# Attention pairs of two batches in one chain with joined biases, w2's splits at other places of a visit, and an opening with its loads and squares in another order

## The chip, the cores and the metric

One core of a Trainium2 chip runs the whole kernel. The metric is the device time of one execution in microseconds (us). The engines are PE (TensorE, matmuls), DVE (VectorE), ACT (ScalarE), POOL (GpSimd) and SP, which issues nearly all DMAs. Each engine works through its own instructions in program order and waits for the others by semaphores.

## What is computed

Random-feature attention for 4 batches of 8 heads (576 positions, 64 dimensions, 128 features), followed by a mixture of 4 experts on the 2304 x 512 result:

```
phi(x) = exp(x omega' - |x|^2/2 - max(...)) / sqrt(m)      x = q, k scaled by 64^-1/4
kv = phi(k)' v,   z = sum phi(k),   attn = phi(q) kv / (phi(q) z + 1e-6)
out = sum over e of p[:, e] * (relu(attn w1[e]) w2[e])     w1: 512x1024, w2: 1024x512
```

All arithmetic is float32. For the expert matmuls each operand is split into two parts, high and low, and three matmuls (high·high, low·high, high·low) make one product.

## The kernel before

**Order by hand.** The emission order of the code is the order on each engine. A tile pool hands out rotating buffers; a tile's buffer is reused when its last emitted reader is done. PSUM has 8 banks in one pool (`bank`), used by everything.

**Batch 0** of the attention is done in `begin` (four head pairs, class `Pair`) and finished in `first_rest`. **Batches 1 to 3** are done by class `Halves`, one pair of heads at a time, by the generator `later_ticks`, cut into ticks. The expert work is a list of visits: half an expert (4 blocks of 128 hidden features, FH = 4) for a range of rows. The first 11 visits (N0 = 11) are on the rows of batch 0 (`first_visit`, `plain`): three for 256 rows, five for 512 rows and, between them, three more for 256 rows. Then 16 visits (`fast`) work on two blocks of 896 rows, 8 visits each; they form the hidden layer with seven products p1 to p7 for each of two groups, 14 products of six 128x448 matmuls, then seven output tiles of 12 matmuls 128x512.

**Pace.** A visit yields shares of work ("units"): 8 for a visit of 512 or 896 rows, 4 for one of 256. `emit` runs ticks of the window's generator at a fixed rate per unit. Window 0 (visits 0 to 2) runs `first_rest` at 14/11 ticks a unit. Window 3 (visits 3 to 10, 52 units) runs batches 1 and 2 at 107/45.4 = 2.36. Window N0 (first 8 fast visits, 64 units) runs batch 3 at 53/(64 x 0.86) = 0.96. In a fast visit all 14 products and the start of three output tiles are one unit, so no tick falls between products.

**A pair's 12 ticks.** 1: project k (two banks `k_ps`), project the tails of k and q (two banks `t_ps`), maxima of k. 2: bias of k (two small DVE operations on 128x8, L293 and L294), four exponentials on ACT (`exp`, L300), lengths of q. 3: four more exponentials, maxima of the tails (L286). 4: project q, bias of k's and q's tails (L293, L294 on 128x1), exponentials of the tails (`exp_tails`, L308), maxima of q. 5, 6: bias and exponentials of q. 7: `sum_keys`, whose first matmul (L317) needs the tail of k. 8 to 12: transposes, numerators, divisions. Loads and squares of the next pair are spread over ticks 5 to 10. In front of a batch's first pair stand 5 opening ticks: loads of k, q, v and the tails of v, an empty tick, the squares on POOL, the lengths on DVE.

**w2.** `load("w2")` brings 128x512 of w2 into one of three buffers `w2r`; `split_w2` makes the high part `w2h` on ACT (L473) and the low part `w2l` on POOL (L476), and then issues the next load on SP. In `begin` two loads are issued ahead, so the loads stay two ahead of the splits for good. `sides` splits w1 for the next visit in the output tiles and issues its loads.

**omega.** `om_r`, a copy of omega for batches 1 to 3, is loaded on SP late in `begin` and scaled on DVE (L901) in the middle of batch 0's last steps.

Of the kernel before, what the change touches and what calls it, by code (L numbers as in the profile page):

```python
# [6 lines left out]
F32 = mybir.dt.float32  # L7
# [7 lines left out]
def attention_moe(ctx, tc, kT, qT, kd, qd, kn, qn, vn, omT, probs, w1, w2, out):  # L15
# [10 lines left out]
    nc = tc.nc  # L26
# [209 lines left out]
    class Halves(Pair):  # L236
# [42 lines left out]
            for j in range(2):  # L279
                nc.vector.tensor_reduce(mx[:, 4 * j:4 * j + 4], ps[j].rearrange("p (i m) -> p i m", m=M), AX.X, ALU.max)  # L280

        def maxima_tails(self):
            for i, which in enumerate("kq"):
                for j in range(2):
                    rows = slice(j * D, (j + 1) * D)
                    nc.vector.tensor_reduce(  # L286
                        getattr(self, "mx" + which)[rows, 8:], self.t_ps[j][rows, i * M:(i + 1) * M], AX.X, ALU.max
                    )

        def bias(self, which, cs):  # L290

            sq, mx, nb = (getattr(self, x + which)[:, cs] for x in ("sq", "mx", "nb"))
            nc.vector.scalar_tensor_tensor(mx, sq, -QS * QS / 2, mx, ALU.mult, ALU.add)  # L293
            nc.vector.scalar_tensor_tensor(nb, sq, -QS * QS / 2, mx, ALU.mult, ALU.subtract)  # L294

# [4 lines left out]
                nc.scalar.activation(f[:, i], ps[:, i * P:(i + 1) * P], AF.Exp, bias=nb[:, 4 * j + i:4 * j + i + 1])  # L300
            (self.kp if which == "k" else self.qx)[j] = f

        def exp_tails(self):
            for i, which in enumerate("kq"):
                f = att.tile([P, 1, M], F32, tag=which + "pt", name=which + "p", bufs=2)
                for j in range(2):
                    rows = slice(j * D, (j + 1) * D)
                    nc.scalar.activation(  # L308
                        f[rows, 0], self.t_ps[j][rows, i * M:(i + 1) * M], AF.Exp, bias=getattr(self, "nb" + which)[rows, 8:]
                    )  # L310
                (self.kp if which == "k" else self.qx)[2] = f

        def sum_keys(self):

# [58 lines left out]
                    own = slice(j * D, (j + 1) * D)  # L373
                    nc.vector.tensor_tensor(raw_x[own, place(self.hp), c:c + m], ps[j][own, o:o + m], dn[own, o:o + m], ALU.mult)

    def later_ticks(b):

        pairs = [Halves(b, hp) for hp in range(NP)]
        pairs[0].load("k")
        pairs[0].load("q")  # L380
        pairs[0].load_v()
        pairs[0].load_tails()
        yield
        yield
        pairs[0].square("k")
        yield
        pairs[0].square("q")
        yield
        pairs[0].lengths("k")
        yield  # L390
        for p, then in zip(pairs, pairs[1:] + [None]):
            p.project("k")
            p.project_tails()
            p.maxima("k")
            yield
            p.bias("k", slice(0, 8))
            p.exp("k", 0)
            p.lengths("q")
            yield
            p.exp("k", 1)  # L400
            p.maxima_tails()
            yield
            p.project("q")
            p.bias("k", slice(8, 9))
            p.bias("q", slice(8, 9))
            p.exp_tails()
            p.maxima("q")
            yield
            p.bias("q", slice(0, 8))
            p.exp("q", 0)  # L410
            if then:
                then.load("k")
            yield
            p.exp("q", 1)
            if then:
                then.load("q")
            yield
            p.sum_keys()
            if then:
                then.load_v()  # L420
                then.square("k")
            yield
            p.turn(0)
            yield
            p.turn(1)
            if then:
                then.square("q")
            yield
            p.numerators(0)
            if then:  # L430
                then.lengths("k")
            yield
            p.divide(0)
            p.numerators(1)
            yield
            p.divide(1)
            yield
# [240 lines left out]
    def fast(v):  # L678

        u, n = visits[v][0], BIG // 2  # L680
        tiles = BIG // P
        hs = [tuple(held([P, 2 * n], x) for x in ("hh", "hl")) for _ in range(FH)]
        P_ = [{}, {}]
        ready = sides(v + 1) if v + 1 < len(visits) else iter(())
        more = build(u + 1) if u == 1 and visits[v + 1][0] == 2 else iter(())

        def product(g, p, where, start=True):
            if start:
                P_[g][where] = bank("g1")[:, :n]
            ps = P_[g][where]  # L690
            (wa, wc), (xa, xc) = W[v, "w1", g][p], X[p]
            for k in range(2):
                w = slice(k * P, (k + 1) * P)
                for a, x, at in ((wa, xa, 0), (wa, xc, 1), (wc, xa, 2)):
                    nc.tensor.matmul(  # L695
                        ps, a[:, w], x[:, k], start=(start and k + at == 0), stop=(k == 1 and at == 2), skip_group_check=not start
                    )

        def keep(g, where, name):
            P_[g][name] = t = held([P, 512], "sum", F32)[:, :n]  # L700
            nc.scalar.activation(t, P_[g][where], AF.Copy)  # L701

        def both(g, f, j, where, name):
            ha, hc = (x[:, j * n:(j + 1) * n] for x in hs[2 * g + f])
            t = P_[g][name]
            nc.vector.tensor_tensor(t, P_[g][where], t, ALU.add)  # L706
            nc.scalar.activation(ha, t, AF.Relu)  # L707
            nc.vector.scalar_tensor_tensor(hc, t, 0.0, f32(ha), ALU.max, ALU.subtract)  # L708

        def p1(g):  # L710
            product(g, 1, "u")
            keep(g, "u", "p1")

        def p2(g):
            product(g, 2, "b2")
            both(g, 0, 0, "b2", "p1")

        def p5(g):
            product(g, 5, "b5")
            keep(g, "b5", "p5")  # L720

        def p6(g):
            product(g, 6, "u", start=False)
            keep(g, "u", "u2")

        def p7(g):
            product(g, 7, "u", start=False)
            both(g, 1, 1, "u", "p5")

        def p4(g):  # L730
            product(g, 4, "u", start=False)
            ha, hc = (x[:, :n] for x in hs[2 * g + 1])
            nc.scalar.activation(ha, P_[g]["u"], AF.Relu)
            nc.vector.scalar_tensor_tensor(hc, P_[g]["u"], 0.0, f32(ha), ALU.max, ALU.subtract)

        def p3(g):
            product(g, 3, "b5", start=False)
            both(g, 0, 1, "b5", "u2")

        g2 = {}  # L740

        def begun(t):
            g2[t] = bank("g2")
            outputs(v, hs, g2[t], t, range(2))

        p1(0)
        split_w2()
        p2(0)
        split_w2()
        p5(0)  # L750
        next(more, None)
        p6(0)
        split_w2()
        p1(1)
        next(more, None)
        p2(1)
        split_w2()
        p7(0)
        next(more, None)
        p5(1)  # L760
        p3(0)
        p4(0)
        next(more, None)
        p6(1)
        next(ready, None)
        begun(0)
        p7(1)
        next(more, None)
        begun(1)
        p3(1)  # L770
        p4(1)
        next(more, None)
        begun(2)
        yield 1
        for t in range(tiles):
            if t in g2:
                outputs(v, hs, g2[t], t, range(2, FH))
            else:
                g2[t] = bank("g2")
                outputs(v, hs, g2[t], t, range(FH))  # L780
            gather(v, g2[t], t)
            next(ready, None)
            next(more, None)
            yield 1
        for _ in more:
            pass

    def begin():
# [84 lines left out]
        keys(3)  # L873
        load("w2")
        load("w2")
        for _ in range(4):
            split_w(nc.gpsimd, nc.gpsimd)
        for p in ps:
# [7 lines left out]
        ps[2].exp("q", 0)  # L886
        ps[3].project("q", 0)
        keys_exp(3)
        for p in ps[:2]:
            p.square("q1", nc.gpsimd)  # L890
        for _ in range(4):
            split_w(nc.gpsimd, nc.gpsimd)

        ps[0].finish(0)
        ps[1].numerators(0)
# [2 lines left out]
        ps[3].exp("q", 0)  # L898

        normalize_probs()  # L900
        nc.vector.tensor_scalar(om_r, om_r, QS, None, ALU.mult)  # L901
        ps[1].finish(0)
        ps[2].numerators(0)
        ps[3].turn(0, nc.vector)
# [25 lines left out]
            split_w(lo=nc.vector)  # L930
            yield 1

    def first_rest(pairs):

        pairs[0].project("q", 1)
        pairs[0].project("q", 2)
# [1 line left out]
        for hp, p in enumerate(pairs):  # L938
# [4 lines left out]
            if hp + 1 < NP:  # L943
                pairs[hp + 1].project("q", 1)
                pairs[hp + 1].project("q", 2)
            yield
            p.turn(1, nc.vector)
            p.turn(2, nc.vector)
            yield
            p.numerators(1)  # L950
            yield
            p.finish(1)
        yield

    def chain(*many):
        for x in many:
            yield from x
# [2 lines left out]

    def emit():
        pairs, g1 = begin()
        windows = {
            0: (first_rest(pairs), 14 / 11),
            3: (chain(later_ticks(1), later_ticks(2)), 107 / 45.4),
            N0: (later_ticks(3), 53 / (NV * (BIG // P + 1) * 0.86)),
        }
        ticks, n, done, per = iter(()), 0, 0.0, 0
        for v in range(len(visits)):
# [70 lines left out]
```

## Time and profile before

| | us |
|---|---|
| median of 3 runs | 946.17 (946.09 to 950.82) |
| the profiled execution's own time | 950.79 |
| its span, first to last instruction | 949.0 |
| PE busy | 912.3 (96%) |
| DVE busy | 571.9 (60%) |
| ACT busy | 433.1 (46%) |
| POOL busy | 379.7 (40%) |
| mean granted clock of TensorE | 0.991 |

A busy PE is one that has a matmul under way; its clock is granted at 2.4 GHz (1.0) or 1.2 GHz (0.5), and a mean between them over a stretch is a mix of the two.

### The profile page before, as it was taken

The page shows a single profiled execution, that of the slowest core. Times are in us where ns is not written, and L with a number is a line of the kernel's source. Part 1 is how long each engine was busy: PE and PEld are TensorE (multiplying, and loading weights), DVE is VectorE, ACT ScalarE, POOL GpSimd, SP SyncE. Part 2 cuts the span into 40 slices and gives each one's busy share as a digit, 9 for nine tenths or more (in the row PEclk, how much of TensorE's full clock was granted, in tenths as well). Part 3 has the DMA queues.
Part 4 walks back from the last instruction along what each step waited for, and adds up shares of the span by engine and source line. Part 5 has one row for each costly group of instructions (what it writes and reads, how often), then busy time and mean ns, then how long its engine had stood idle before and what let it go on. Part 6 is the DMA issues. An engine that isn't in the chain of part 4 may idle for free.

```text
span 949.0 us, 13220 instructions
## 1 busy us (share of the span) xinstructions
PE 912.3 (96%) x4892; PEld 784.8 (83%) x4892; DVE 571.9 (60%) x993; ACT 433.1 (46%) x964; POOL 379.7 (40%) x296
## 2 busy tenths in 40 slices
PE   7799998998999989999999999999999999999998
PEld 7788787877877868888888888888788888888886
DVE  5464577767887846648486576677535545545443
ACT  5354565545666445444534435353443343342430
POOL 3736444353543434332343524244344343343330
PEclk9999999999999989999999999999999999999999
DMA  6534535255331333121311302114022031021102
GB/s 169 143 112 145 157 117 184 71 155 164 126 129 34 97 103 114 59 67 26 125 56 59 126 5 85 35 54 155 24 78 68 23 89 66 24 89 56 45 12 77
DMA packets 47361, 83.56 MB, mean 88 GB/s; under 512 B 8705, under 2 KB 17089, under 8 KB 47297
## 3 DMA queue, kind: packets, MB, share of 16 engines
q1 hardware_dynamic: 47056, 82.43, 28.1%
q8 instruction: 38, 0.62, 0.3%
q10 hardware_dynamic: 240, 0.30, 0.1%
q14 instruction: 27, 0.21, 0.1%
HBM read 77.99 MB, written 4.72 MB: 87 GB/s over the span
## 4 chain that ended last, share of the span: by engine, by line
PE 59%; DVE 4%; issue 2%; ACT 1%; DMA 1%; POOL 1%; SPq 0%; ACTq 0%; POOLq 0%
PE g L695 26%; PE g L579 10%; PE g L581 10%; PE g L580 10%; DMA w2r<-in_w 1%; DVE acc L592 1%; PE kv L321 1%; POOL w1sl L476 1%; PE qt_ps L332 0%; DVE sum L706 0%; DVE xbl L476 0%; DVE dn L370 0%; DVE mxk L293 0%; ACT xbh L473 0%; PE k_ps L266 0%
## 5 line engine op out<-in xcount | busy, mean ns | idle before, releaser
L579 PE MATMUL g<-w2h,hh 128*128 128x512 f32 x536 | 213.1, 397 | 1.9 <-ACT hh L570 1.0
L581 PE MATMUL g<-w2h,hl 128*128 128x512 f32 x536 | 209.8, 391 | 0.5 <-DVE hl L571 0.5
L580 PE MATMUL g<-w2l,hh 128*128 128x512 f32 x536 | 209.2, 390 | 0.0
L476 POOL TENSOR_TENSOR w2l<-w2r,w2h 128x512 fp32r<-128x512 f32 x93 | 122.9, 1328 | 142.0 <-ACT w2h L473 100.0
L476 POOL TENSOR_TENSOR w1sl<-w1r,w1sh 128x1024 fp32r<-128x1024 f32 (+1 forms) x59 | 113.4, 1922 | 159.9 <-ACT w1sh L473 158.6
L476 POOL TENSOR_TENSOR w1al<-w1r,w1ah 128x256 fp32r<-128x256 f32 (+1 forms) x77 | 82.2, 1085 | 164.4 <-ACT w1ah L473 162.3
L706 DVE TENSOR_TENSOR sum<-g,sum 128x448 f32<-128x448 f32 x96 | 59.7, 622 | 126.5 <-PE g L695 109.6
L592 DVE SCALAR_TENSOR_TENSOR acc<-g,pr,acc 128x512 f32<-128x512 f32 x126 | 93.9, 747 | 64.8 <-PE g L581 63.8
L581 PEld LDWEIGHTS g<-w2h,hl 128*128 128x128 f32 x536 | 100.6, 188 | 24.4 <-DVE hl L571 1.9
L579 PEld LDWEIGHTS g<-w2h,hh 128*128 128x128 f32 x536 | 101.0, 188 | 22.9 <-ACT hh L570 1.7
L580 PEld LDWEIGHTS g<-w2l,hh 128*128 128x128 f32 x536 | 100.9, 188 | 18.5
L707 ACT ACTIVATE hh<-sum 128x448 fp32r<-128x448 f32 x96 | 55.5, 578 | 120.4 <-DVE sum L706 120.4
L708 DVE SCALAR_TENSOR_TENSOR hl<-sum,hh 128x448 fp32r<-128x448 f32 x96 | 61.9, 645 | 61.9 <-ACT hh L707 61.9
L695 PE MATMUL g<-xbh,w1sh 128*128 128x448 f32 x256 | 94.3, 368 | 1.5 <-ACT sum L701 1.5
L473 ACT ACTIVATE w1sh<-w1r 128x1024 fp32r<-128x1024 f32 (+1 forms) x59 | 51.3, 870 | 93.9 <-DVE w1r L530 93.8
L695 PE MATMUL g<-xbl,w1sh 128*128 128x448 f32 x256 | 94.2, 368 | 0.0
L695 PE MATMUL g<-xbh,w1sl 128*128 128x448 f32 x256 | 93.8, 367 | 0.0
L695 PE MATMUL g<-xbh,w1ah 128*128 128x448 f32 x192 | 71.1, 370 | 6.1 <-DVE sum L706 6.1
L701 ACT ACTIVATE sum<-g 128x448 f32<-128x448 f32 x96 | 51.4, 539 | 53.1 <-PE g L695 52.9
L695 PE MATMUL g<-xbh,w1al 128*128 128x448 f32 x192 | 70.7, 368 | 0.0
L695 PE MATMUL g<-xbl,w1ah 128*128 128x448 f32 x192 | 70.5, 367 | 0.0
L473 ACT ACTIVATE w2h<-w2r 128x512 fp32r<-128x512 f32 x90 | 55.9, 629 | 22.6 <-DMA w2r<-in_w 22.0
(158 smaller groups left out, 1632.8 us busy)
## 6 DMA issues: line engine op xcount, KB each, us to landing
w1r<-in_w SPq DMA_DIRECT2D x54, 512.0 KB, 3.6
w2r<-in_w SPq DMA_DIRECT2D x108, 256.0 KB, 2.7
out<-acc SPq DMA_DIRECT2D x18, 256.0 KB, 2.7
va<-in_vn SPq DMA_DIRECT2D x14, 256.0 KB, 4.8
k<-in_kd SPq DMA_DIRECT2D x12, 288.0 KB, 3.6
k<-in_kn SPq DMA_DIRECT2D x12, 288.0 KB, 4.8
q<-in_qd SPq DMA_DIRECT2D x12, 288.0 KB, 5.2
q<-in_qn SPq DMA_DIRECT2D x12, 288.0 KB, 5.5
```

What stands on the lines that cost most here:

```text
L321: nc.tensor.matmul(kv[:, cs], self.kp[j][:, t], va[:, t, cs], start=False, stop=(j == 1 and t == 3))
L473: hi.activation(a, t, AF.Copy)
L476: lo.tensor_tensor(c, t, f32(a), ALU.subtract)
L579: nc.tensor.matmul(ps, ha[:, ts_], wa, start=(c == 0), stop=False)
L580: nc.tensor.matmul(ps, ha[:, ts_], wc, start=False, stop=False)
L581: nc.tensor.matmul(ps, hc[:, ts_], wa, start=False, stop=(c == FH - 1))
L592: nc.vector.scalar_tensor_tensor(acc[i], ps, sc, acc[i], ALU.mult, ALU.add)
L695: nc.tensor.matmul(ps, a[:, w], x[:, k], start=(start and k + at == 0), stop=(k == 1 and at == 2), skip_group_check=not start)
L701: nc.scalar.activation(t, P_[g][where], AF.Copy)
L706: nc.vector.tensor_tensor(t, P_[g][where], t, ALU.add)
L707: nc.scalar.activation(ha, t, AF.Relu)
L708: nc.vector.scalar_tensor_tensor(hc, t, 0.0, f32(ha), ALU.max, ALU.subtract)
```

## The change

It has four parts. Batches 1 and 2 become one chain of eight pairs, so that the last pair of batch 1 loads and squares the first pair of batch 2; the opening is a generator of its own, of six ticks, which runs inside `first_rest` for batch 1 and at the head of window N0 for batch 3. In a pair, the tail of k gets its maxima, bias and exponentials with the rest of k, the tail of q with the rest of q, and each bias is one joined 128x9 operation. In `fast` the four `split_w2` stand behind p1(0), p5(0), p7(0) and p4(0), where they stood behind p1(0), p2(0), p6(0) and p2(1). In `begin` a third `load("w2")` is issued ahead, two of the splits go ahead of the squares of q1, and the scaling of `om_r` moves to `first_rest`.

```
-            p.bias("k", slice(0, 8))
+            p.maxima_tails("k")
+            p.bias("k")
             p.exp("k", 0)
             p.lengths("q")
             yield
             p.exp("k", 1)
-            p.maxima_tails()
+            p.exp_tails("k")
+            p.maxima_tails("q")
             yield
             p.project("q")
-            p.bias("k", slice(8, 9))
-            p.bias("q", slice(8, 9))
-            p.exp_tails()
             p.maxima("q")
             yield
-            p.bias("q", slice(0, 8))
+            p.bias("q")
             p.exp("q", 0)
             if then:
                 then.load("k")
             yield
             p.exp("q", 1)
+            p.exp_tails("q")
...
             p.sum_keys()
             if then:
                 then.load_v()
+                if then.hp == 0:
+                    then.load_tails()
                 then.square("k")
...
+    def opening(p):
+        p.load("k")
+        yield
+        p.load("q")
+        yield
+        p.load_v()
+        p.load_tails()
+        yield
+        p.square("k")
+        yield
+        p.square("q")
+        yield
+        p.lengths("k")
+        yield
...
         p1(0)
         split_w2()
         p2(0)
-        split_w2()
         p5(0)
         next(more, None)
+        split_w2()
         p6(0)
-        split_w2()
         p1(1)
         next(more, None)
         p2(1)
-        split_w2()
         p7(0)
         next(more, None)
+        split_w2()
         p5(1)
         p3(0)
         p4(0)
+        split_w2()
...
         load("w2")
         load("w2")
+        load("w2")
         for _ in range(4):
             split_w(nc.gpsimd, nc.gpsimd)
...
-        for p in ps[:2]:
-            p.square("q1", nc.gpsimd)
-        for _ in range(4):
+        for _ in range(2):
             split_w(nc.gpsimd, nc.gpsimd)
+        ps[0].square("q1", nc.gpsimd)
+        for _ in range(2):
+            split_w(nc.gpsimd, nc.gpsimd)
+        ps[1].square("q1", nc.gpsimd)
...
         normalize_probs()
-        nc.vector.tensor_scalar(om_r, om_r, QS, None, ALU.mult)
         ps[1].finish(0)
...
-    def first_rest(pairs):
+    def first_rest(pairs, then):
...
+            if hp:
+                next(then, None)
             yield
             p.turn(1, nc.vector)
             p.turn(2, nc.vector)
+            if hp == 0:
+                nc.vector.tensor_scalar(om_r, om_r, QS, None, ALU.mult)
             yield
             p.numerators(1)
+            if hp:
+                next(then, None)
...
+        later = [Halves(b, hp) for b in range(1, B) for hp in range(NP)]
         windows = {
-            0: (first_rest(pairs), 14 / 11),
-            3: (chain(later_ticks(1), later_ticks(2)), 107 / 45.4),
-            N0: (later_ticks(3), 53 / (NV * (BIG // P + 1) * 0.86)),
+            0: (first_rest(pairs, opening(later[0])), 14 / 11),
+            3: (later_ticks(later[:-NP]), 97 / 45.4),
+            N0: (chain(opening(later[-NP]), later_ticks(later[-NP:])), 54 / (NV * (BIG // P + 1) * 0.8)),
         }
```

## Rows read from the trace of the kernel before

**Rows 1.** The page: busy us, share of the span, instructions of each engine.
```profile
PE 912.3 (96%) x4892; PEld 784.8 (83%) x4892; DVE 571.9 (60%) x993; ACT 433.1 (46%) x964; POOL 379.7 (40%) x296
```
**Rows 2.** Waits, whole span: engine, line, releaser: us in total, times, longest.
```profile
ACT sum L473 <- DMA w2r<-in_w: 7.1, 3, 3.2
PE kv L317 <- ACT kp L308: 7.4, 5, 2.7
...
PE g L695 <- DVE sum L706: 6.1, 2, 4.4
...
PE k_ps L146 <- ACT k L137: 4.6, 1, 4.6
...
PE x_ps L224 <- DVE xt L215: 4.4, 1, 4.4
...
PE g L695 <- ACT sum L701: 1.5, 2, 1.3
...
PE t_ps L273 <- DMA q<-in_qd: 1.3, 1, 1.3
PE g L564 <- ACT kp L300: 1.3, 1, 1.3
...
PE g L579 <- ACT hh L570: 1.0, 1, 1.0
...
PE g L579 <- ACT kp L300: 0.8, 1, 0.8
```
**Rows 3.** Windows of four stretches and a visit without attention: length, busy us, granted clock.
```profile
41.00:45.00 4.00, 3.84 (x19) 3.61 (x18) 1.58 (x6) 0.38 (x1) 3.84 (x5) 0.57 0.43 131
160.00:165.00 5.00, 5.00 (x24) 4.63 (x25) 1.98 (x5) 4.05 (x13) 0.69 (x1) 0.66 0.87 317
219.00:223.00 4.00, 4.00 (x19) 3.69 (x18) 1.12 (x2) 3.46 (x11) 1.28 (x1) 0.57 0.91 309
336.70:342.00 5.30, 5.28 (x14) 4.68 (x15) 2.41 (x4) 2.19 (x5) 0.65 (x1) 0.51 1.00 320
700.00:736.00 36.00, 36.00 (x170) 31.43 (x169) 17.82 (x29) 13.39 (x24) 13.92 (x10) 1.00 0.18 56
```
**Rows 4.** Timeline at om_r's scaling: start, us, engine, line, [idle before <- releaser].
```profile
33.77 0.23 DVE L87 TENSOR_TENSOR pr<-pr,prs 128x72 f32<-128x72 f32 x1
39.05 0.55 DVE L901 TENSOR_SCALAR om_r<-om_r 128x128 f32<-128x128 f32 x1 [5.05 <-DMA om_r<-in_omT]
...
40.79 0.44 PE L224 MATMUL x_ps<-ident,xt 128*128 128x128 f32 x2 [4.45 <-DVE xt L215]
```
**Rows 5.** Timeline of one pair's exponentials, 152 to 161 us.
```profile
154.34 2.17 ACT L300 ACTIVATE kp<-k_ps,nbk 128x128 f32<-128x128 f32 x8 [2.55 <-DVE nbk L294]
...
157.65 1.23 DVE L293 SCALAR_TENSOR_TENSOR mxk<-sqk,mxk 128x1 f32<-128x1 f32 x1
...
159.11 0.74 ACT L308 ACTIVATE kp<-t_ps,nbk 64x128 f32<-64x128 f32 x2 [1.58 <-DVE nbk L294]
...
159.90 0.70 PE L317 MATMUL kv<-vb,kp 128*128 128x256 f32 x2 [2.56 <-ACT kp L308]
```
**Rows 6.** Groups by line and shape, DVE, whole span: busy us, mean ns.
```profile
L286 DVE TENSOR_REDUCE mxk<-t_ps 64x1 f32<-64x128 f32 x24 | 6.8, 284 | 0.2
L293 DVE SCALAR_TENSOR_TENSOR mxk<-sqk,mxk 128x1 f32<-128x1 f32 x12 | 8.0, 667 | 0.2
```
**Rows 7.** Timeline at the start of the first fast visit, 323 to 337 us.
```profile
326.76 0.34 SPq L469 DMA_DIRECT2D w1r<-in_w  x1
328.10 7.37 SPq L469 DMA_DIRECT2D w2r<-in_w  x4
...
326.84 0.61 ACT L473 ACTIVATE w2h<-w2r 128x512 fp32r<-128x512 f32 x1
...
333.15 0.63 ACT L473 ACTIVATE w2h<-w2r 128x512 fp32r<-128x512 f32 x1 [4.82 <-DMA w2r<-in_w]
...
336.72 0.74 PE L695 MATMUL g<-xbh,w1ah 128*128 128x448 f32 x1 [4.43 <-DVE sum L706]
```

More of the change, by code (lines that the diff above doesn't have):

```diff
@@ L280, in maxima, with maxima_tails, bias @@
                 nc.vector.tensor_reduce(mx[:, 4 * j:4 * j + 4], ps[j].rearrange("p (i m) -> p i m", m=M), AX.X, ALU.max)
[L282 to L292, printed above, removed]
+        def maxima_tails(self, which):
+            for j in range(2):
+                rows, cs = slice(j * D, (j + 1) * D), slice("kq".index(which) * M, ("kq".index(which) + 1) * M)
+                nc.vector.tensor_reduce(getattr(self, "mx" + which)[rows, 8:], self.t_ps[j][rows, cs], AX.X, ALU.max)
+        def bias(self, which):
+            sq, mx, nb = (getattr(self, x + which) for x in ("sq", "mx", "nb"))
             nc.vector.scalar_tensor_tensor(mx, sq, -QS * QS / 2, mx, ALU.mult, ALU.add)
@@ L301, in exp, with exp_tails @@
             (self.kp if which == "k" else self.qx)[j] = f
[L303 to L311, printed above, removed]
+        def exp_tails(self, which):
+            f = att.tile([P, 1, M], F32, tag=which + "pt", name=which + "p", bufs=2)
+            for j in range(2):
+                rows, cs = slice(j * D, (j + 1) * D), slice("kq".index(which) * M, ("kq".index(which) + 1) * M)
+                nc.scalar.activation(f[rows, 0], self.t_ps[j][rows, cs], AF.Exp, bias=getattr(self, "nb" + which)[rows, 8:])
+            (self.kp if which == "k" else self.qx)[2] = f
         def sum_keys(self):
@@ L374, in divide, with later_ticks @@
                     nc.vector.tensor_tensor(raw_x[own, place(self.hp), c:c + m], ps[j][own, o:o + m], dn[own, o:o + m], ALU.mult)
[L376 to L382, printed above, removed]
+    def opening(p):
+        p.load("k")
         yield
+        p.load("q")
         yield
-        pairs[0].square("k")
+        p.load_v()
+        p.load_tails()
         yield
-        pairs[0].square("q")
+        p.square("k")
         yield
-        pairs[0].lengths("k")
+        p.square("q")
         yield
+        p.lengths("k")
+        yield
+    def later_ticks(pairs):
         for p, then in zip(pairs, pairs[1:] + [None]):
```

## The prediction, as put on record before the run

> **What bounds the kernel now.** I read the page first: PE has a matmul under way for 912.3 us of a span of 949.0, and no other engine passes 60% [rows 1]. So the time is the 36.7 us in which PE stood still, what its clock lost, and PE's work. Where nothing disturbs it PE is the bound: a late stretch of 36 us, a fast visit without attention, has PE busy for all 36.00 us at full clock although DVE, ACT and POOL are each busy less than half of it [rows 3]. Nothing in the change touches such a stretch: it adds and removes no matmul. A gain can only come out of PE's waits, so the second view is the list of waits, PE's lines alone [rows 2]. About 4.6 us is the first input at the very start and stays, and some 3.6 us at the end (the last sum and store, the end of the span behind PE's last matmul) stays too. The rest has four large causes: `kv L317` waiting for the tail of k's exponentials (7.4 us, 5 times), the products `g L695` waiting for DVE's sum (6.1, twice), the transposes `x_ps L224` waiting for `xt` (4.4, once), and 1.3 for the first load of q. Third, the granted clock: after the longer of these waits it stands at a mean of 0.51 to 0.66 in stretches of 4 to 5.3 us in which PE is busy [rows 3]. That is time at 1.2 GHz in place of 2.4, and it is lost on top of the wait.
>
> The sum below is made on the profiled execution, 950.8 us (span 949.0 and 1.8 around it). It is the slowest of the three runs, 4.6 above their median. No row says what the others did not suffer; nearly all large waits and clock losses are terms of the sum, so I expect the difference to shrink with them and take the sum for the median.
>
> **om_r's scaling leaves the opening.** DVE is done with `pr` at 33.77 + 0.23 = 34.0, then waits 5.05 us for the DMA of `om_r`, and all of `finish` and `numerators` queues behind it; PE stands 4.45 us for `xt` [rows 4]. Taken out, DVE is ready 5 us earlier and `xt` comes before PE runs dry: 4.4 gained. The scaling itself, 0.55 us, goes to `first_rest`, some 20 us later, when the load has long landed, and is needed only by batch 1. Behind the wait, from 41 to 45 us, the clock was 0.57: 4 x 0.43 = 1.7 us, gained too. Next in line are the squares of q1 on POOL; they now alternate with splits, and the squares are needed by PE only in the first visit. Term: 6.1 (bounds 3, if POOL's q1 takes over part, to 6.8).
>
> **The opening of batch 1 moves to window 0.** Seven issues on SP, two squares on POOL and one reduction on DVE go ahead of loads and splits of visits 1 to 3. Gone are PE's wait for q (1.3) and the one for `hh` (1.0), where ACT was held by that pair's late bias [rows 2]: 2.3. Against it stands that some 1.5 MB now competes with w1 and w2; what it meets is ACT's waits for w2r (7.1 us, 3 times, longest 3.2 [rows 2]), and none of them reached PE. I count nothing; bound, one wait of 3.2.
>
> **Tail of k with k.** In one pair the exponentials of k run from 154.34 to 156.51; then ACT waits 1.58 us until DVE, behind other work and with a bias operation on 128x1 that took 1.23 us, has the tail's bias; the tail's exponentials take 0.74 and PE starts `kv` at 159.90 after 2.56 us idle, so from 157.34 [rows 5]. In the new order the joined bias needs the two maxima of k's tail first, 2 x 0.284 = 0.57 us [rows 6], and the tail's exponentials follow at once: 156.51 + 0.57 + 0.74 = 157.82. Left is 157.82 - 157.34 = 0.5 of 2.56, so four fifths are gained: 0.8 x 7.4 = 5.9. Ends: 0, if the wait only moves to another bank or engine, and 7.4, as six ticks now take 6/2.14 = 2.81 units in place of 6/2.36 = 2.55. I take 5.9. The clock losses at 160 to 165 (5 x 0.34 = 1.7) and 219 to 223 (4 x 0.43 = 1.7) follow such waits and go: 3.4. Half of the small bias operations vanish, up to 0.667 us of DVE each [rows 6]; DVE is not the bound, so nothing.
>
> **One chain.** At the seam of the batches, loads, squares and bias of a first pair came in a bunch, and a hidden product waited 1.3 us for the exponentials of k (`g L564` [rows 2]). With the loads spread over the pair before, that goes: 1.3 (bounds 0 and 1.3). The ticks of batch 3 get denser, 1.055 for 0.963 a unit; its known waits (1.5 and 0.8 [rows 2]) may grow by that tenth: 0.2, nothing.
>
> **w2.** At the start of the first fast visit SP issues the next w2r only at 328.10, behind w1r at 326.76; ACT reaches the third split with its data not there, waits 4.82 us until 333.15, the relus queue behind it, and PE stands 4.43 us until 336.72 [rows 7]. The second such wait brings `g L695` to 6.1 in all [rows 2]. With three loads ahead the third split has its data before the visit begins, and only the fourth depends on a load issued in the visit. That one is now the first behind 328.10 and lands when the third did, by 333.15; the fourth split stands behind ten products. A product is some 1.2 us (by columns the 14 products are 0.47 of the 36 us of a visit); the second split, behind the second product, ran at 326.84 [rows 7], so the fourth, eight products on, comes at about 336. Both waits go: 6.1. The clock of 336.7 to 342 gives 5.3 x 0.49 = 2.6. Later use is no danger: four more products and three half tiles, some 9 us, lie between the fourth split and its first reader. The price of the third load is that SP waits for the split whose buffer it refills, as it already does for w1; behind it stand the loads of attention and w1, at most one POOL operation later. Term: 8.7 (bounds 4.4, only the large wait, and 8.7).
>
> **What it adds.** `t_ps` is held until tick 6, not 4. From tick 4 to 6 four of eight banks (`q_ps`, `t_ps`) are taken, as from tick 1 to 3 in both versions. What such a shortage costs is seen at `g L564` and `g L579` waiting for `kp`: 1.3 and 0.8, once each in 12 pairs [rows 2]. I take the same again, 2.1; ends 0 and one of 1.3 for each pair, 15.6.
>
> The Trainium skill, Perfetto Trace Analysis, section "Optimization Strategy", says that the same bubble coming back on the engine that should be saturated can mean too little PSUM for the next tile; "Matmul Optimizations" there asks that all eight banks be put to use. By that rule the longer hold would be paid in every pair, which is the second rival below; the trace so far shows it in 2 of 12.
>
> **Sum.** 6.1 + 2.3 + 5.9 + 3.4 + 1.3 + 8.7 = 27.7 off, 2.1 on: 950.8 - 25.6 = 925.
>
> **Rivals.** (1) *The attention's waits move.* With DVE still late, hidden products or queries wait where `kv` waited; om_r and w2 gain alone: 950.8 - 6.1 - 2.3 - 8.7 + 2.1 = 936. For it: ACT's start on k hangs on DVE's bias before and after. Against: the wait was the tail's, behind a second trip through DVE. (2) *Banks in every pair.* 15.6 in place of 2.1: 938.5. (3) *Slower, by banks and clock.* If PE runs out of banks between ticks 4 and 6 for as long as it did at `kv` (2.6) in each pair, the clock falls each time too (1.7): 12 x 4.3 = 51.6, in all 950.8 - 27.7 + 51.6 = 975. It decides from the seventh pair on: 7 x 4.3 = 30 is more than 27.7. Against it: ticks 1 to 3 hold as many banks already. (4) *No change.* w2's load is still late because SP is, and the attention's waits move with their clock: 8.7 + 5.9 + 3.4 = 18.0 of the terms lost, 950.8 - 27.7 + 18.0 + 2.1 = 943.
>
> **Chances.** Forecast 0.60, waits move 0.17, banks 0.11, no change 0.07, slower 0.05. The forecast's own range is 917 (the bounds' good ends: 3.1 more than the sum, the 2.1 not paid, and half of the runs' 4.6) to 931 (opening 3, w2 4.4 short). To leave out no more than 2 in 10 the range takes in the first two rivals: 917 to 939. A measurement of this kernel tells about 0.5% (4.7 us) from no change. Faster than 941.4: forecast and the first two rivals, 0.88; within: 0.07; slower than 950.9: 0.05.
>
> **What would show it.** In the changed profile: no wait of DVE at `om_r` and PE without a gap between 34 and 45 us; `kv L317` waiting for `kp` under 2.5 us in all; no wait of 1 us or more of `g L695` for a sum at the first visit of either row block; the clock at 1.0 but for at most two short stretches; PE idle some 15 us in all. A list of `g` or `kv` waits for `qp` or `kp` of over 10 us would show the banks; a wait of ACT's fourth split for w2r with PE behind it would show the load still late. The forecast fails if PE's idle stays over 25 us.

## The result and the profile after

| | before | after |
|---|---|---|
| median, us | 946.73 (4 runs, 946.09 to 950.82) | 921.21 (4 runs, 920.35 to 921.76) |
| ratio | | 0.9721 (0.9692 to 0.9750) |
| profiled execution, us | 950.79 | 921.18 |
| span, us | 949.0 | 919.4 |
| PE idle in the span, us | 36.7 | 17.0 |

The kernel before has one run more here than in the time and profile before. The change makes the kernel 2.8% faster. The page of the kernel after, engines and granted clock by slice, answers to [rows 1]:

```profile
PE 902.4 (98%) x4892; PEld 779.5 (85%) x4892; DVE 551.2 (60%) x945; ACT 431.4 (47%) x964; POOL 379.1 (41%) x296
...
PEclk9999999999999999999999999999999999999999
```

PE has the same 4892 matmuls and stands still 919.4 - 902.4 = 17.0 us in place of 36.7. Its busy time fell by 9.9 us as well. Matmuls at half clock last longer, and the four stretches at half clock of [rows 3], gone now, make up 1.7 + 1.7 + 1.7 + 2.6 = 7.7 us of it; where the rest went was not traced. Most lines of the code moved up by 1 to 6: `g L695` is now L694, `kv L317` L311, `qt_ps L332` L326, `g L579` L578; `om_r`'s scaling went from L901 to L953. The waits of the kernel after (in total, times, longest), to be read beside [rows 2]:

```profile
ACT qp L297 <- DVE nbq L291: 26.3, 11, 4.5
...
DVE mxq L285 <- ACT kp L304: 22.4, 12, 4.0
...
PE k_ps L146 <- ACT k L137: 4.6, 1, 4.6
...
PE qt_ps L326 <- ACT qp L297: 2.2, 3, 1.3
PE kv L173 <- ACT kp L161: 1.6, 2, 1.3
PE nd L356 <- DVE qtl L337: 1.2, 3, 0.8
PE g L580 <- DVE hl L570: 0.8, 2, 0.5
PE g L694 <- ACT kp L297: 0.8, 1, 0.8
PE g L694 <- ACT sum L700: 0.7, 2, 0.5
```

PE's three large lines of [rows 2] are gone: `kv` for the tail of k, the fast products for DVE's sum, and `x_ps` for `xt`. What is left of PE's list is the first input and some small waits. The two lines at the top are new in size: ACT waits 26.3 us for the bias of q, where it waited 11.4 us in 11 waits before, and DVE waits 22.4 us for ACT's exponentials of k's tail, a wait that the kernel before doesn't have. The experiments take them up again.

Windows of the kernel after (length, busy us of PE, PEld, DVE, ACT, POOL, granted clock, DMA share, GB/s), the opening, the first fast visit and the late stretch of [rows 3]:

```profile
41.00:45.00 4.00, 4.00 (x33) 3.65 (x32) 3.28 (x7) 2.84 (x9) 3.22 (x3) 1.00 0.31 104
...
306.00:340.00 34.00, 33.82 (x172) 28.67 (x171) 21.70 (x32) 16.98 (x32) 18.61 (x13) 1.00 0.45 135
700.00:736.00 36.00, 36.00 (x169) 31.45 (x168) 17.89 (x29) 13.41 (x24) 13.94 (x10) 1.00 0.20 58
```

The undisturbed stretch is as it was; the other two are now like it, with the clock at 1.00. DVE's timeline in the opening of the kernel after (start, us), beside [rows 4]:

```profile
34.39 0.23 DVE L87 TENSOR_TENSOR pr<-pr,prs 128x72 f32<-128x72 f32 x1
34.63 0.42 DVE L232 TENSOR_TENSOR xl<-x_ps,xh 128x256 fp32r<-128x256 f32 x1
...
48.42 0.22 DVE L953 TENSOR_SCALAR om_r<-om_r 128x128 f32<-128x128 f32 x1
```

Behind `pr` DVE goes straight on; the scaling runs 14 us later without a wait. SP and ACT at the first fast visit of the kernel after, beside [rows 7]:

```profile
307.93 0.34 SPq L468 DMA_DIRECT2D w1r<-in_w  x1
...
309.31 8.22 SPq L468 DMA_DIRECT2D w2r<-in_w  x4
...
308.42 0.62 ACT L472 ACTIVATE w2h<-w2r 128x512 fp32r<-128x512 f32 x1
...
312.95 0.61 ACT L472 ACTIVATE w2h<-w2r 128x512 fp32r<-128x512 f32 x1
...
315.18 0.62 ACT L472 ACTIVATE w2h<-w2r 128x512 fp32r<-128x512 f32 x1
```

SP still issues w2r late and slowly (8.22 us for four issues), but no split waits for it: the last three, shown here, run at 308.42, 312.95 and 315.18 with no idle time that a DMA ended.

### The profile page after: what moved, and what is told of

Read it like the earlier page. It is cut to its first block, busy times and chain, and to the rows that moved or that the text cites. A ratio compares the mean times of both kernels' runs of the same rounds, so it can differ in the third digit from the quotient of the medians.

```text
span 919.4 us, 13210 instructions
## 1 busy us (share of the span) xinstructions
PE 902.4 (98%) x4892; PEld 779.5 (85%) x4892; DVE 551.2 (60%) x945; ACT 431.4 (47%) x964; POOL 379.1 (41%) x296
## 4 chain that ended last, share of the span: by engine, by line
PE 79%; DVE 10%; ACT 6%; issue 2%; DMA 1%; POOL 1%; SPq 0%; ACTq 0%; DVEq 0%; POOLq 0%
PE g L694 28%; PE g L578 12%; PE g L580 12%; PE g L579 12%; DVE dn L364 2%; PE g L563 2%; PE g L564 2%; PE g L565 2%; PE kv L315 2%; DVE acc L591 1%; ACT qp L297 1%; DVE raw_x L368 1%; PE q_ps L266 1%; ACT kp L297 1%; PE k_ps L266 1%
## 5 line engine op out<-in xcount | busy, mean ns | idle before, releaser
L578 PE MATMUL g<-w2h,hh 128*128 128x512 f32 x536 | 212.6, 397 | 0.0
L579 PE MATMUL g<-w2l,hh 128*128 128x512 f32 x536 | 209.0, 390 | 0.0
L578 PEld LDWEIGHTS g<-w2h,hh 128*128 128x128 f32 x536 | 100.7, 188 | 20.8 <-issue 1.4
L579 PEld LDWEIGHTS g<-w2l,hh 128*128 128x128 f32 x536 | 100.8, 188 | 18.6
L694 PE MATMUL g<-xbh,w1sh 128*128 128x448 f32 x256 | 93.7, 366 | 0.7 <-ACT sum L700 0.7
L694 PE MATMUL g<-xbl,w1sh 128*128 128x448 f32 x256 | 93.7, 366 | 0.0
L694 PE MATMUL g<-xbh,w1sl 128*128 128x448 f32 x256 | 93.4, 365 | 0.0
L694 PE MATMUL g<-xbh,w1ah 128*128 128x448 f32 x192 | 70.6, 368 | 0.8 <-ACT kp L297 0.8
L694 PE MATMUL g<-xbh,w1al 128*128 128x448 f32 x192 | 70.3, 366 | 0.0
L694 PE MATMUL g<-xbl,w1ah 128*128 128x448 f32 x192 | 70.1, 365 | 0.0
```

The source lines that it names most:

```text
L578: nc.tensor.matmul(ps, ha[:, ts_], wa, start=(c == 0), stop=False)
L579: nc.tensor.matmul(ps, ha[:, ts_], wc, start=False, stop=False)
L694: nc.tensor.matmul(ps, a[:, w], x[:, k], start=(start and k + at == 0), stop=(k == 1 and at == 2), skip_group_check=not start)
```

## The experiments

Each kernel is timed against the kernel before on the same chip. One table holds them all. "First fast product" is where the first matmul of `g L695` (or its new line) starts: opening, batches 1 and 2, and visits 0 to 10 lie ahead of it. "From there" is the time to the start of the last matmul. The last column is span less PE's busy time. The profiled execution of the kernel before was 4.1 us above its median; as its fast visits take much the same as in the other kernels with the old w2 (622.2 to 624.7), this seems to lie in its 320.8.

| kernel | median, us | ratio to before | first fast product | from there | PE idle |
|---|---|---|---|---|---|
| before | 946.73 | 1 | 320.8 | 624.2 | 36.7 |
| before + om_r's scaling moved | 944.71 | 0.9949 (0.9927 to 0.9971) | 316.4 | 623.6 | 34.9 |
| before + w2 (load and places) | 937.84 | 0.9894 (0.9873 to 0.9915) | 316.0 | 614.9 | 26.0 |
| before + tails and joined biases | 946.56 | 0.9981 (0.9968 to 0.9994) | 315.7 | 624.7 | 33.2 |
| before + chain, opening and paces | 933.99 | 0.9849 (0.9827 to 0.9870) | 304.9 | 622.2 | 25.3 |
| after | 921.21 | 0.9721 (0.9692 to 0.9750) | 301.9 | 613.5 | 17.0 |
| after, once more | 921.54 | 0.9723 (0.9687 to 0.9759) | 303.8 | 613.7 | 18.1 |
| after - third load | 922.94 | 0.9738 (0.9705 to 0.9771) | 303.0 | 614.6 | 18.9 |
| after - new places | 924.45 | 0.9754 (0.9721 to 0.9788) | 301.5 | 617.4 | 18.7 |
| after - tails and joined biases | 917.70 | 0.9681 (0.9642 to 0.9721) | 297.6 | 614.5 | 15.7 |
| after - wider pace | 930.55 | 0.9803 (0.9783 to 0.9823) | 311.5 | 613.6 | 23.2 |
| after - one chain | 924.54 | 0.9739 (0.9721 to 0.9757) | 304.9 | 613.7 | 18.5 |
| after, banks held longer | 923.06 | 0.9726 (0.9705 to 0.9747) | 303.5 | 613.4 | 20.4 |
| after - om_r's scaling moved | 926.51 | 0.9762 (0.9741 to 0.9783) | 306.8 | 613.5 | 20.5 |

### One part alone, in the kernel before

**om_r's scaling.**

```
         normalize_probs()
-        nc.vector.tensor_scalar(om_r, om_r, QS, None, ALU.mult)
...
     def first_rest(pairs):
...
+            if hp == 0:
+                nc.vector.tensor_scalar(om_r, om_r, QS, None, ALU.mult)
```

> The kernel before, with the scaling of om_r alone moved to first_rest. By the prediction's first term DVE no longer waits 5.05 us, PE's 4.45 us wait for xt and the clock loss of 1.7 us behind it go: 946.7 - 6.1 = 940.6. Rival, the time is passed on: POOL, which still squares q1 ahead of w2's splits, becomes what the first visit waits for, and the gain is under 3 us (944 or more), with a new PE wait between 36 and 60 us.

Measured: 0.9949, some 4.8 us. The wait for `xt` is gone, but another one came some 8 us later. PE's timeline of this kernel (idle before and its releaser in brackets):

```profile
48.97 1.38 PE L206 MATMUL nd<-kvs,qt 128*128 128x65 f32 x8 [1.43 <-DVE qt L198]
```

The window behind it, in the same kernel:

```profile
49.60:53.00 3.40, 3.40 (x13) 2.92 (x12) 2.46 (x8) 0.00 (x0) 0.58 (x1) 0.51 0.94 302
```

PE waited 1.43 us for DVE, and the clock stood at 0.51 for 3.4 us behind it. What made DVE late is seen in its timeline in this kernel:

```profile
45.31 1.35 DVE L476 TENSOR_TENSOR w1sl<-w1r,w1sh 128x512 fp32r<-128x512 f32 x1
...
46.91 1.40 DVE L476 TENSOR_TENSOR w1sl<-w1r,w1sh 128x512 fp32r<-128x512 f32 x1
```

The same two splits in DVE's timeline of the kernel after:

```profile
46.08 0.69 DVE L475 TENSOR_TENSOR w1sl<-w1r,w1sh 128x512 fp32r<-128x512 f32 x1
...
47.02 0.68 DVE L475 TENSOR_TENSOR w1sl<-w1r,w1sh 128x512 fp32r<-128x512 f32 x1
```

These two splits take twice as long where POOL has an operation under way: in this kernel POOL's last split of w2 runs from 44.80 to 46.10 and a square of q1 from 46.19 to 47.77; in the kernel after POOL is done at 44.30. The Trainium skill, SBUF — State Buffer, section "SBUF: two separate sides", says that a DVE operation with two SBUF inputs and a GpSimd operation that reads SBUF exclude one another for the whole of an instruction; the trace agrees, with 1.35 and 1.40 us beside POOL and 0.69 and 0.68 without. So the order of splits and squares on POOL, which the prediction left without a price, probably shares in the gain of the opening. It was not run by itself, so its share is not shown.

**w2.**

```
         p2(0)
-        split_w2()
         p5(0)
...
+        split_w2()
         p6(0)
-        split_w2()
...
         p2(1)
-        split_w2()
         p7(0)
...
+        split_w2()
         p5(1)
         p3(0)
         p4(0)
+        split_w2()
...
         load("w2")
         load("w2")
+        load("w2")
```

> The kernel before, with the third w2 load ahead and the new places of the four splits alone. By the prediction both waits of the products for DVE's sum (4.4 and 1.7 us) and the clock loss of 2.6 behind the first go: 946.7 - 8.7 = 938.0. Rival: the loads stay late because SP is held behind w1, so a later split waits and the time is within 2 us of before. A second rival: the gain is 4.4 alone, 942.

Measured: 0.9894, some 10 us. PE waits for no sum of DVE at the fast products, and the fast visits take 614.9 in place of 624.2 us: 9.3 us, all of them in the stretch that the edit touches.

**The tails of k and q, and joined biases**, the edit to `maxima_tails`, `bias` and `exp_tails` of the diff above, with the order of ticks 2 to 6:

```
-            p.bias("k", slice(0, 8))
+            p.maxima_tails("k")
+            p.bias("k")
...
-            p.maxima_tails()
+            p.exp_tails("k")
+            p.maxima_tails("q")
...
-            p.bias("k", slice(8, 9))
-            p.bias("q", slice(8, 9))
-            p.exp_tails()
...
-            p.bias("q", slice(0, 8))
+            p.bias("q")
...
+            p.exp_tails("q")
```

> The kernel before, with the tail of k handled with k, the tail of q with q and the joined biases alone (two chains, old pace, old w2, om_r where it was). By the prediction kv's waits for the tail of k fall from 7.4 to 1.5 us and the clock losses at 160 and 219 us go: 946.7 - 9.3 = 937.4. Rival, banks: t_ps is held two ticks longer, hidden products wait for exponentials instead, and the time is 944 or more. If only the waits fall and the clock does not come back, 940.8.

Measured: 0.9981, some 1.8 us where 9.3 were expected. The waits of this kernel:

```profile
ACT qp L297 <- DVE nbq L291: 27.1, 11, 5.1
...
DVE mxq L285 <- ACT kp L304: 20.9, 11, 4.0
...
PE qt_ps L326 <- ACT qp L297: 3.3, 4, 1.4
...
PE kv L311 <- ACT kp L304: 1.3, 3, 0.5
```

The wait at `kv` did fall from 7.4 to 1.3 us, and the clock is at 1.00 where the prediction had two losses:

```profile
160.00:165.00 5.00, 5.00 (x28) 4.09 (x27) 3.39 (x7) 4.88 (x13) 2.92 (x3) 1.00 0.89 307
215.00:223.00 8.00, 6.51 (x34) 5.30 (x35) 4.89 (x9) 6.53 (x18) 5.89 (x5) 1.00 0.69 234
```

In its place PE waits 3.3 us for the exponentials of q, and the two lines of DVE and ACT that the kernel after shows are here too. They belong to this part. What they cost PE is more than its list of waits says: from the first projection of batch 1 to the first fast product, counted from the start of one matmul to the start of the next, the transposes of q hold PE for 12.9 us and the numerators behind them for 15.4, where they take 8.9 and 13.1 in the kernel before.

**The chain, the opening in window 0 and the paces.**

```
...
-            0: (first_rest(pairs), 14 / 11),
-            3: (chain(later_ticks(1), later_ticks(2)), 107 / 45.4),
-            N0: (later_ticks(3), 53 / (NV * (BIG // P + 1) * 0.86)),
+            0: (first_rest(pairs, opening(later[0])), 14 / 11),
+            3: (later_ticks(later[:-NP]), 97 / 45.4),
+            N0: (chain(opening(later[-NP]), later_ticks(later[-NP:])), 54 / (NV * (BIG // P + 1) * 0.8)),
```

> The kernel before, with the chain of eight pairs, the opening in window 0, the wider pace of ticks and batch 3's new opening and pace alone (old biases and tails, old w2, om_r where it was). By the prediction PE's waits for the first q (1.3), for hh (1.0) and for k's exponentials at the seam (1.3) go: 946.7 - 3.6 = 943.1. Rival: most of kv's waits come from the bunching of ticks and from the seam, not from the order of the tails, and the chain alone takes them too: 946.7 - 3.6 - 7 = 936 or less, with kv waiting under 2 us.

Measured: 0.9849, some 14.3 us where 3.6 were expected. The waits of this kernel, whose tails are those of the kernel before:

```profile
ACT qp L300 <- DVE nbq L294: 13.1, 10, 3.1
...
PE g L700 <- DVE sum L711: 6.1, 2, 4.4
...
PE kv L317 <- ACT kp L308: 1.3, 2, 0.9
PE qt_ps L332 <- ACT qp L300: 0.8, 2, 0.4
```

The wait at `kv` fell to 1.3 us with the old tails and nothing moved to the transposes. So this part alone does what the tails' edit was credited with.

The four gains add up to 4.8 + 10.1 + 1.8 + 14.3 = 31.0 us; the whole change brings 0.0279 x 946.7 = 26.4. The 4.6 us too much are hardly more than the intervals allow: some 2 us either way for each gain but the tails' 1.2, and 2.8 for the whole. If they are real, either two parts remove the same wait, as the tails and the chain both do at `kv`, or one part costs something beside the others. The next runs take the parts out one at a time.

### One part undone, in the kernel after

**The kernel after, once more**, as the measure for the three that follow, with which it shared the chip.

> The changed kernel itself, unaltered, on the chip of the next three runs, so that they are compared with it and not with a time from another chip. Expected 0.972 of the kernel before, as in its own timing, with no wait of PE over 1.5 us behind the first 31 us.

Measured: 0.9723, 921.54 us (919.51 to 923.31).

**Two loads ahead.** The third `load("w2")` in `begin` is taken out.

```
         load("w2")
         load("w2")
-        load("w2")
```

> The changed kernel with two loads of w2 ahead in place of three, the new places of the splits kept. By the prediction it is the third load that has the third split's data there; the third split now stands behind p7(0), four products or 4.9 us later than the old one behind p6(0) in program order, the old wait was 4.8, so the places alone may cover most of it: 0 to 2 us over the changed kernel. If the places do nothing, the waits of 4.4 and 1.7 and the clock behind them come back: 8.7 over it.

Measured: 0.9738. With the new places alone one split of a fast visit waits for w2, the fourth of the first, and PE's longest wait behind it in that visit is 0.32 us. ACT's timeline:

```profile
315.61 0.64 ACT L472 ACTIVATE w2h<-w2r 128x512 fp32r<-128x512 f32 x1 [1.44 <-DMA w2r<-in_w]
```

The rest of what came back lies in the opening, POOL's timeline and PE's:

```profile
39.06 0.61 POOL L474 CAST w2h<-w2r 128x512 fp32r<-128x512 f32 x1 [2.37 <-DMA w2r<-in_w]
...
44.67 1.38 PE L146 MATMUL q_ps<-om,q 128*128 128x128 f32 x10 [1.51 <-POOL q L139]
```

The 1.4 us to the kernel after are within both intervals.

**The old places, with three loads ahead.** The four splits stand behind p1(0), p2(0), p6(0) and p2(1) again.

```
         p2(0)
+        split_w2()
         p5(0)
...
-        split_w2()
         p6(0)
+        split_w2()
...
         p2(1)
+        split_w2()
         p7(0)
...
-        split_w2()
         p5(1)
         p3(0)
         p4(0)
-        split_w2()
```

> The changed kernel with three loads ahead and the splits at their old places, behind p1(0), p2(0), p6(0) and p2(1). The third split's data is there before the visit; the fourth's load lands some 5 us after it is issued, about where the third's did, and the fourth split now stands two products later than the third did, 2.4 us: a wait of some 2 us is left at the first visit of a row block, one of which reaches PE: 1 to 4 us over the changed kernel. Rival: the third load alone is enough, within 0.5 us.

Measured: 0.9754, 2.9 us more than the kernel after beside it. ACT's timeline at the fourth split of the first fast visit:

```profile
314.25 0.63 ACT L472 ACTIVATE w2h<-w2r 128x512 fp32r<-128x512 f32 x1 [2.98 <-DMA w2r<-in_w]
```

PE's timeline behind it:

```profile
318.36 0.51 PE L578 MATMUL g<-w2h,hh 128*128 128x512 f32 x1 [2.10 <-ACT hh L732]
```

The fast visits take 617.4 us: 3.7 more than with the new places, 6.8 less than in the kernel before. So either half of the edit covers most of the late load, the places more of it than the third load.

**The old tails and separate biases.** The edit of the third kernel above in reverse; the chain, w2 and the opening stay as in the kernel after.

```
-            p.maxima_tails("k")
-            p.bias("k")
+            p.bias("k", slice(0, 8))
...
-            p.exp_tails("k")
-            p.maxima_tails("q")
+            p.maxima_tails()
...
+            p.bias("k", slice(8, 9))
+            p.bias("q", slice(8, 9))
+            p.exp_tails()
...
-            p.bias("q")
+            p.bias("q", slice(0, 8))
...
-            p.exp_tails("q")
```

> The changed kernel with the old order of the tails and the separate biases, all else kept. The chain alone took most of kv's waits (1.3 us left of 7.4), the tails alone moved the time by 0.2%. If the two overlap, the tails are worth little on top of the chain: 1 to 3 us over the changed kernel, kv waiting 1 to 2 us. If the tails are worth in the chain what the prediction gave them, 9 us over. If holding t_ps to tick 6 costs, it is faster than the changed kernel.

Measured: 0.9681, 917.70 us (917.19 to 918.05): 3.8 us faster than the kernel after beside it, no run of the one within the runs of the other, and the fastest kernel of this study. Its page, the line of the engines:

```profile
PE 900.4 (98%) x4892; PEld 778.4 (85%) x4892; DVE 568.2 (62%) x993; ACT 432.2 (47%) x964; POOL 378.2 (41%) x296
```

Its waits:

```profile
ACT qp L300 <- DVE nbq L294: 13.1, 10, 3.1
...
PE kv L317 <- ACT kp L308: 0.8, 1, 0.8
PE qt_ps L332 <- ACT qp L300: 0.8, 2, 0.4
```

DVE has 17 us more to do than in the kernel after, in 48 more instructions, and the kernel is faster: DVE's total was not the limit. The expectation's third case came true, but its reason, the banks of `t_ps`, is spoken against by the run that holds them longer, below. DVE's wait for ACT (22.4 us) is gone from the list. What the new order does is seen in one pair of the kernel after (the run beside this one) between 194 and 202 us. DVE's timeline:

```profile
195.24 0.68 DVE L285 TENSOR_REDUCE mxq<-t_ps 64x1 f32<-64x128 f32 x2 [1.88 <-ACT kp L304]
```

ACT's:

```profile
194.83 0.76 ACT L304 ACTIVATE kp<-t_ps,nbk 64x128 f32<-64x128 f32 x2
...
199.17 1.14 ACT L297 ACTIVATE qp<-q_ps,nbq 128x128 f32<-128x128 f32 x4 [2.41 <-DVE nbq L291]
```

PE's:

```profile
201.63 0.59 PE L326 MATMUL qt_ps<-ident,qp 128*128 128x128 f32 x2 [1.30 <-ACT qp L297]
```

The maxima of q's tail only read the PSUM tile `t_ps`, as ACT's exponentials of k's tail do, but they stand behind those: DVE idles 1.88 us until the first of ACT's two is over. Behind that stand the accumulation of a product, the maxima of q and the joined bias; ACT then waits 2.41 us for that bias and PE 1.30 us for the exponentials. That the tails' edit costs 3.8 us is shown. That this chain is how, is read from the trace: a kernel with the tails of k and q in PSUM tiles of their own was not run, and of the 5.1 us by which the stretch from the first projection of batch 1 to the first fast product differs (215.3 and 210.2), PE's idle time explains 5.2 - 2.4 = 2.8. Where the 5.1 us lie is clear: counted from the start of one matmul to the start of the next, the transposes hold PE for 10.9 us in that stretch of the kernel after and 8.1 here, the numerators for 15.5 and 13.2, and all other matmuls together differ by 0.1.

**The old pace.** 107 for 97 ticks in the 45.4 units, for the same 96 ticks.

```
-            3: (later_ticks(later[:-NP]), 97 / 45.4),
+            3: (later_ticks(later[:-NP]), 107 / 45.4),
```

> The changed kernel with batches 1 and 2 at the old pace of 107/45.4 ticks a unit in place of 97/45.4; the 96 ticks are then done 4.7 units earlier. If the wider pace is what took kv's waits, they come back in part, as waits for kp or qp, 3 us and more with a clock loss or two: 4 to 8 us over the changed kernel. If it was the seam and the opening, under 1.5 us over it.

Measured: 0.9803, 0.8% or some 8 us more than the kernel after. All of it lies ahead of the first fast product (311.5 against 301.9 and 303.8). One of PE's waits in its timeline:

```profile
220.62 0.73 PE L326 MATMUL qt_ps<-ident,qp 128*128 128x128 f32 x2 [1.45 <-ACT qp L297]
```

The window around it, in the same kernel:

```profile
220.00:225.00 5.00, 4.38 (x16) 3.49 (x17) 2.38 (x4) 3.80 (x11) 3.65 (x3) 0.66 0.45 130
```

**Two batches one after the other**, with the six opening ticks of batch 2 between them again (103 for 102 ticks).

```
-            3: (later_ticks(later[:-NP]), 97 / 45.4),
+            3: (chain(later_ticks(later[:NP]), opening(later[NP]), later_ticks(later[NP:-NP])), 103 / 45.4),
```

The ticks fill the same 45.4 units, so that this kernel differs from the kernel after by the seam and by a pace 6% denser.

> The changed kernel with a seam again: batch 1's four pairs, then the six opening ticks of batch 2, then its four pairs, at 103/45.4 ticks a unit so that they end where they did. Pace and seam together are what the chain changed. By the prediction the seam alone costs 1.3 us at a hidden product. With the pace of 2.27, between the old 2.36 and the new 2.14, 2 to 5 us over the changed kernel; if only the seam counts, a wait of 1 to 3 us between 195 and 220 us and nothing elsewhere.

Measured: 0.9739, some 1.6 us more than the kernel after and within its interval. So a pace 6% denser and a seam cost 1.6 us together, where a pace 10% denser cost 8: the price does not look like one that grows evenly with the pace. A change of pace also moves each tick to another place among a visit's products; no run keeps the pace and moves the ticks, so that this counts, and not the spacing, is a rival left open.

One of PE's waits in its timeline, as long as the one above, and the window behind it:

```profile
251.07 0.59 PE L326 MATMUL qt_ps<-ident,qp 128*128 128x128 f32 x2 [1.45 <-ACT qp L297]
...
251.00:256.00 5.00, 4.93 (x28) 4.15 (x29) 2.78 (x6) 4.21 (x13) 3.21 (x3) 1.00 0.76 253
```

**Banks held two ticks longer.** q's tail has its exponentials in tick 8, so `t_ps` is held until then.

```
             p.exp("q", 1)
-            p.exp_tails("q")
...
             p.turn(0)
+            p.exp_tails("q")
             yield
             p.turn(1)
```

> The changed kernel with the tail of q's exponentials two ticks later, behind the first transposes, so that the two banks of t_ps are held from tick 1 to tick 8: the suspected cost, doubled. By the prediction banks cost little (2.1 us for the two ticks of the change): 0 to 3 us over the changed kernel. If a shortage of banks is paid in every pair, 12 waits of 1.3 us, 15 us over, or more with the clock.

Measured: 0.9726, the same as the kernel after. No hidden product waits for an exponential of q, but the transposes of q's tail, which need what was moved, do:

```profile
PE qt_ps L330 <- ACT qp L304: 5.4, 6, 1.5
```

Other waits went in exchange, those of the numerators (`nd L356`, 1.2 us in the kernel after) among them. So this kernel differs by more than the hold, and its time is that of both together; no other wait in PE's list is for the exponentials that free `t_ps`.

**om_r's scaling back in the opening.**

```
         normalize_probs()
+        nc.vector.tensor_scalar(om_r, om_r, QS, None, ALU.mult)
...
-            if hp == 0:
-                nc.vector.tensor_scalar(om_r, om_r, QS, None, ALU.mult)
```

> The changed kernel with the scaling of om_r back in the opening. By the prediction DVE waits 5 us again, PE 4.4, and the clock costs 1.7: 6.1 over the changed kernel, where moving it alone in the kernel before gave 0.5%. If 4.4 is what the wait is worth and the clock falls by chance, 4.4 to 4.8.

Measured: 0.9762, some 4 us more than the kernel after by the ratios. PE's timeline:

```profile
39.12 0.44 PE L224 MATMUL x_ps<-ident,xt 128*128 128x128 f32 x2 [3.63 <-DVE xt L215]
```

## Why the prediction was right, and where it was not

The time is 921.2 us, 3.8 under the forecast of 925 and within the forecast's own range, whose ends were added up a little wrongly: the stated good ends give 0.7 + 1.5 = 2.2 in place of 3.1, the bad ones some 932 in place of 931. The list of waits, the clock and PE's idle time (17.0 us, some 15 foretold) came out as described: no wait at `om_r`, none of 1 us at a fast product for a sum, none listed at `kv L311`, and the clock at 1.00. But it credited two of its terms wrongly. The waits at `kv` and the clock behind them were real and did go, only by another part of the change: the tails' term and the chain with the opening were foretold at 9.3 + 3.6 = 12.9 us, and the chain's part alone brings 14.3. That the sum came out so near in spite of it is luck.

**om_r's scaling: right, somewhat smaller.** 4.8 us alone and some 4 when undone, for 6.1; within its bounds of 3 to 6.8. The lower bound's reason, POOL's squares and splits next in line, is what the run of the part alone met: 1.43 us of waiting and 3.4 us of half clock came back a little later. That POOL is what made DVE late there is read from the trace.

**w2: right.** 10.1 us by the ratio and 9.3 in the fast visits, for 8.7. The step gave the third load as the reason for the third split and the new place as that for the fourth. Undone one at a time they cover for one another: without the third load the visits lose 0.9 us, without the places 3.7.

**Tail of k with k: this step failed.** It took 5.9 us of waiting and 3.4 of clock as gained. At `kv` that is what happened, but alone the edit brings 1.8 us, and within the whole change it costs 3.8. The step followed the tail of k alone. The tail of q moved too, and its maxima now stand on DVE behind ACT's exponentials of k's tail, and ahead of q's own maxima and bias; the transposes and numerators that need q's exponentials take PE 5.0 us longer in the kernel after than without the edit. The first rival had the form of this ("the attention's waits move"), but for the whole change it fell: 936 was forecast for it.

**One chain: under-sized.** The term was 1.3 us, with 2.3 for the opening's move. The part alone brings 14.3 us. Of it the pace is some 8, by the run with the old pace in the kernel after; the rest, opening and seam, was not taken further apart, but for the seam's 1.6. The prediction had the pace's numbers (2.81 units for six ticks in place of 2.55) and used them only as the reason for the upper end of the tails' term. With more of a visit's products between two ticks, DVE and ACT have more time until PE comes to the next one, and several of a pair's waits shrink at once: with the old pace in the kernel after, PE waits 4.1 us for `qth` at `nd L354` and 3.4 for `qp` at `qt_ps L326`, in the kernel after 0.3 and 2.2. That it is the spacing, and not the places that the ticks come to, is argued.

**What it adds: not paid.** The prediction read one row in two ways, the 1.3 us at `g L564`: as a wait of the seam, which goes, and as the price of a shortage of banks, which comes again. It stayed with the tails alone (`g L558`, 1.3 us) and went with the chain, which fits the first reading. No 2.1 us for banks is seen: holding them two ticks longer yet gives 0.9726 for 0.9723, though that run changes other waits too. The time itself ends the second and the third rival. The Trainium skill, Perfetto Trace Analysis, section "Optimization Strategy", says that a bubble that keeps coming back on the engine that should be saturated can mean too little PSUM. In these runs it did not: the longer hold cost nothing, and the bubbles that came back ended with late exponentials (2.2 us at `qt_ps L326`). What was paid instead was DVE's wait for ACT at `t_ps`, which the prediction did not look at, as it took DVE for no bound. The fourth rival, no change, fell with the w2 run.

## What to carry to other kernels

When a change alters how densely side work is spread between matmuls, price that first: it moves many waits of that work at once, and a reordering credited with the same waits may have nothing left to gain. Run each part alone and take each out of the whole; the sum of the single gains can't tell an overlap from a part that does harm, but here taking the parts out did, and leaving one out gave the fastest kernel. Follow every instruction that a reordering moves, those of an engine that is half idle too: what counts is which instruction it stands behind.

## What the runs showed of the hardware

The granted clock fell to half for 3.4 us behind waits of PE as short as 1.43 us (before + om_r's scaling) and 1.45 us (old pace), which cost up to 3.4 x 0.49 = 1.7 us more than the wait. But it stayed at 1.00 behind a wait of 1.45 us in the kernel with the seam (at 251.07), of 1.50 us with the banks held longer (at 152.97), of 1.77 us in before + w2 (at 157.74) and of 1.31 us in the kernel after (at 200.08). So in these runs the length of one wait did not tell whether the clock would fall. DVE's maxima and ACT's exponentials of other columns of one PSUM tile, both only reading it, ran one after the other in the programs as built: DVE waited 22.4 us in 12 waits. Whether the chip would let them run at once no run shows.
